# A gate, three edge columns and one step: reordering ScalarE in the opening of a fused forward and backward kernel

## The chip, the cores and the metric

One core of a Trainium2 chip runs the whole kernel. The metric is device time in microseconds, the median of several executions. TensorE (PE in the profile) multiplies matrices and writes to PSUM; ScalarE (ACT) and VectorE (DVE) read PSUM and work elementwise; GpSimd (POOL) and SyncE (SP) mostly issue transfers here. [...]

## The reference

A layer with two branches, mixed by a gate, and its gradients. `x` has 2048 rows of 1024, the inner width `F` is 3584, everything is bfloat16.

```python
g = sigmoid((x * gate_w).sum(-1, keepdims=True))       # one number per row
X = rfft2(x);  a = irfft2(X * (w_r + 1j * w_i))        # spectral branch
h = x @ w1 + b1;  r = relu(h);  b = (r * r) @ w2 + b2  # dense branch
out = g * a + (1 - g) * b
# returned: out and, for a given grad_out, the gradients of
# x, w_r, w_i, w1, b1, w2, b2 and gate_w
```

## The kernel before

The rows are worked on in 16 tiles of 128 rows. In the opening TensorE makes `h` in groups of eight matmuls (`ph`, L747): ScalarE applies Relu (`rT`, L748) and the square (`h2T`, L749). Then it makes the gradient of the square, also in groups of eight (`pd`, L755), which VectorE multiplies with `2 rT` (`dhT`, L759). `ph` and `pd` share two PSUM banks in the opening, so a group of matmuls can start only when the group before the last has been read.

```python
def bank(name):
    drawn[0] += 1
    return banks[drawn[0] // 2 % len(banks)].tile([P, SW], FP32, name=name, tag="ph", bufs=2)

def hidden(fc, ss, w1g, h2T, rT):
    ph = bank("ph")
    for dc in range(DC):                      # eight matmuls
        opened(mm(ph[:], lhsT=w1g[...], rhs=xT[:, dc, ss], ...), fc)
    nc.scalar.activation(rT[:], ph[:], ACT.Relu, bias=b1col[:, fc : fc + 1])
    nc.scalar.activation(h2T, rT[:], ACT.Square)
```

The gate needs one weighted sum for each row. VectorE makes it for each tile as the rows land (`weigh`, L666, into `gsum`). For four tiles at a time ScalarE makes `1 - g` (`omg`) and `g` (`gcol`), and VectorE scales four tiles of the incoming gradient with `omg`, which TensorE then transposes (`turn_grad`, L647) for the gradient products.

```python
def gate(i0):
    c_ = slice(i0, i0 + 4)
    nc.scalar.activation(omg[:, c_], gsum[:, c_], ACT.Sigmoid, scale=-1.0)   # L675
    nc.scalar.activation(gcol[:, c_], gsum[:, c_], ACT.Sigmoid)              # L676
    for i in range(i0, i0 + 4):
        later["scaled"] = nc.vector.tensor_scalar(out=dbn[:, i, :], in0=dbn[:, i, :], scalar1=omg[:, i : i + 1], ...)
        after(later["scaled"], later["copied"], mybir.DependencyClass.NoSync)
```

The spectral branch begins beside all this. Each tile of `x`, loaded once more (`src`), is folded: sums and differences of its halves (`uv`), then of its quarters (`f`). VectorE does the wide parts, ScalarE three narrow copies of edge columns (L263, L265, L269). Then TensorE multiplies along the rows (`pk`, L277) and along the columns (`pu`, L310).

```python
def folds(fb, xt, earlier=None):
    uv = fb.tile([P, 2, H], FDT, name="uv", tag="uv", bufs=2)
    after(V(out=uv[:, 0, :], in0=xt[:, 0:H], in1=xt[:, H:D], op=ALU.add), earlier, mybir.DependencyClass.NoSync)
    after(V(out=uv[:, 1, :], in0=xt[:, 0:H], in1=xt[:, H:D], op=ALU.subtract), earlier, mybir.DependencyClass.NoSync)
    f = fb.tile([P, 6, Q + 2], FDT, name="f", tag="f", bufs=2)
    ...                                                                        # L261, L262: VectorE
    nc.scalar.copy(out=f[:, 3:0:-2, 0], in_=uv[:, 1, 0 : Q + 1 : Q])           # L263
    nc.scalar.copy(out=f[:, 0:3:2, 0 : Q + 1 : Q], in_=uv[:, 0:1, 0 : Q + 1 : Q].to_broadcast([P, 2, 2]))   # L265
    ...                                                                        # L267, L268: VectorE
    nc.scalar.copy(out=f[:, 5, P::-P], in_=f[:, 0:3:2, P])                     # L269
    return f

def first_stage_of_x():
    f, ft = {0: folds(f1, xs[0], later["last"])}, {}
    for i in range(NT + 1):
        ...
        ft[i] = row_stage(f1, f[i], kf[:], later["last"]);  yield              # pk
        ...                                                                    # pu of tile i - 1, folds of i + 1
        yield
```

`after(a, b, NoSync)` tells the scheduler that `a` comes after `b`; no semaphore is added. The scheduler then chooses the order on each engine. The opening is 32 units, four blocks of eight: eight groups `ph` for rows 0 to 1023, eight groups `pd`, and the same for rows 1024 to 2047.

```python
for u in range(32):
    for i in before.get(u, ()): turn_x(i)               # holds the row sums
    for i in grads_before.get(u, ()): turn_grad(i)
    next(units)                                         # one group ph or pd
    if u in (6, 15, 19):
        gate({6: 4, 15: 8, 19: 12}[u])
    if u == 17:
        for n in range(3): xs[n] = source(n, x_perm)
        stage = first_stage_of_x()
    if u > 19 and u % 2:
        next(stage)
...
total = 22 + 2 * (NT + 4) + 14 + 5 + 4 * R1 + 2 + LEAD + 4 * NT    # steps of side work left after the opening
```

In the rest of the kernel the spectral work runs as side work between the large products: its steps are dealt out at a rate that is worked out from `total`.

Of the kernel before, what the change touches and what calls it, by code (L numbers as in the profile page):

```python
# [10 lines left out]
P = 128  # L11
# [4 lines left out]
ACT = mybir.ActivationFunctionType  # L16
# [108 lines left out]
LEAD = 8  # L125
# [15 lines left out]
def kernel(  # L141
# [22 lines left out]
    nc = tc.nc  # L164
# [8 lines left out]
    R1, R2 = g.R1, g.R2  # L173
    NT = S // P
    Q, H, LW, W1 = D // 4, D // 2, g.Df + 1, g.Df
# [18 lines left out]
    def pool(name, side="left", space=SBUF, stack=None, bufs=1):  # L194
        stack = ExitStack() if stack is None else stack
        kw = {} if space == DRAM else dict(side=side, reuse_waits="tile")
        return stack.enter_context(tc.tile_pool(name=name, bufs=bufs, space=space, **kw)), stack
# [10 lines left out]
    gcol, omg, gpg, bGo, dsc = (cols(n, [NT]) for n in ("gcol", "omg", "gpg", "bGo", "dsc"))  # L208
    gsum = cols("gsum", [NT])
# [24 lines left out]
    def after(ins, earlier, wait=mybir.DependencyClass.Sync):  # L234

        if earlier is not None:
            info = mybir.DependencyInfo(wait, mybir.DependencyReason.DATA)
            tc.add_manual_dep(ins.ins, earlier.ins.name, info, reason="paced")
# [12 lines left out]
    tps, tps_s = pool("tps", "right", PSUM)  # L251


    def folds(fb, xt, earlier=None):
        uv = fb.tile([P, 2, H], FDT, name="uv", tag="uv", bufs=2)
        after(V(out=uv[:, 0, :], in0=xt[:, 0:H], in1=xt[:, H:D], op=ALU.add), earlier, mybir.DependencyClass.NoSync)
        after(V(out=uv[:, 1, :], in0=xt[:, 0:H], in1=xt[:, H:D], op=ALU.subtract), earlier, mybir.DependencyClass.NoSync)

        f = fb.tile([P, 6, Q + 2], FDT, name="f", tag="f", bufs=2)
        a0, a1 = uv[:, :, 1:Q], uv[:, :, H - 1 : Q : -1]  # L260
        V(out=f[:, 0:2, 1:Q], in0=a0, in1=a1, op=ALU.add)  # L261
        V(out=f[:, 2:4, 1:Q], in0=a0, in1=a1, op=ALU.subtract)  # L262
        nc.scalar.copy(out=f[:, 3:0:-2, 0], in_=uv[:, 1, 0 : Q + 1 : Q])  # L263

        nc.scalar.copy(out=f[:, 0:3:2, 0 : Q + 1 : Q], in_=uv[:, 0:1, 0 : Q + 1 : Q].to_broadcast([P, 2, 2]))  # L265
        b0, b1 = f[:, 0:3:2, 0:P], f[:, 0:3:2, Q:P:-1]
        V(out=f[:, 4:6, 0:P], in0=b0, in1=b1, op=ALU.add)  # L267
        V(out=f[:, 4:6, P:Q], in0=b0, in1=b1, op=ALU.subtract)  # L268
        nc.scalar.copy(out=f[:, 5, P::-P], in_=f[:, 0:3:2, P])  # L269
        return f  # L270

    def row_stage(fb, f, kmat, earlier=None):
        pk = fps.tile([P, 8, P], FP32, name="pk", tag="ps2", bufs=2)
        even = [(row, slice(o, o + P)) for row, o in ((5, P), (4, 0), (4, P), (5, 0))]
        odd = [(row, slice(o, Q, 2)) for row, o in ((3, 0), (3, 1), (1, 1), (1, 0))]
        for b, (row, o) in enumerate(even + odd):
            first_ = mm(pk[:, b, :], lhsT=f[:, row, o], rhs=kmat[:, b // 6, :], start=True, stop=True)  # L277
            if b == 0:
                after(first_, earlier, mybir.DependencyClass.NoSync)
        ft = fb.tile([P, 8, P], FDT, name="ft", tag="ft", bufs=2)  # L280
        nc.scalar.copy(out=ft[:], in_=pk[:])
        return ft

    def first_columns(fb, cf, T, i, ft, earlier=None):
        pu = fps.tile([P, 2, H], FP32, name="pu", tag="ps2", bufs=2)
        column_stage(pu, ft, cf, earlier)

        u = fb.tile([P, D], FDT, name="u", tag="u", bufs=2)
        w = fb.tile([P, 2, 2, 2, P // 2], FDT, name="w", tag="w", bufs=2)
        nc.scalar.copy(out=w[:].rearrange("p c x g i -> p (c x g i)"), in_=pu[:, 1, :])  # L290
        uv = u[:].rearrange("p (c h g i) -> p c h g i", c=2, h=2, g=4)
        even = pu[:, 0, :].rearrange("p (g c h i) -> p c h g i", g=2, c=2, h=2)
        nc.scalar.copy(out=uv[:, 0, :, 0::2, :], in_=even[:, 0])
        nc.scalar.mul(out=uv[:, 1, :, 0::2, :], in_=even[:, 1], mul=flip[:])  # L294

        X, Y = (w[:, :, x] for x in range(2))
        V(out=uv[:, :, 0, 1::2, :], in0=X, in1=Y, op=ALU.add)
        V(out=uv[:, :, 1, 3::-2, ::-1], in0=X, in1=Y, op=ALU.subtract)
        rows_of(st, z_scr, T, i, u, True)
# [325 lines left out]
    later = {}  # L625
    f1, f1_s = pool("f1", "right")

    cf = f1.tile(list(consts["cf"].shape), FDT, name="cf", tag="cf")
    xs = {}
# [5 lines left out]
    def source(i, view, earlier=None, tag="src"):  # L635
        src = f1.tile([P, D], BF16, name=tag, tag=tag, bufs=8 if tag == "xsrc" else 4)
        loaded = ld(out=src[:], in_=view[i])
        if earlier is None:
            queued(loaded)
        after(loaded, earlier)  # L640
        return src
# [30 lines left out]
    def gate(i0):  # L672

        c_ = slice(i0, i0 + 4)
        nc.scalar.activation(omg[:, c_], gsum[:, c_], ACT.Sigmoid, scale=-1.0)  # L675
        nc.scalar.activation(gcol[:, c_], gsum[:, c_], ACT.Sigmoid)  # L676
        for i in range(i0, i0 + 4):
            later["scaled"] = nc.vector.tensor_scalar(out=dbn[:, i, :], in0=dbn[:, i, :], scalar1=omg[:, i : i + 1], scalar2=None, op0=ALU.mult)
            after(later["scaled"], later["copied"], mybir.DependencyClass.NoSync)

    def first_stage_of_x():
        f, ft = {0: folds(f1, xs[0], later["last"])}, {}
        for i in range(NT + 1):
            if i + 3 < NT:
                xs[i + 3] = source(i + 3, x_perm, later["last"])
            if i < NT:
                ft[i] = row_stage(f1, f[i], kf[:], later["last"])
                yield
            if i > 0:
                first_columns(f1, cf, 0, i - 1, ft[i - 1], later["last"])  # L690
            if i + 1 < NT:
                f[i + 1] = folds(f1, xs[i + 1], later["last"])
            yield
# [23 lines left out]
    def mlp_in():  # L717
# [9 lines left out]
# [3 lines that stand above are left out]
# [9 lines left out]
        def opened(ins, fc):  # L739
            if fc < 4:  # L740
                after(ins, later["turned"], mybir.DependencyClass.NoSync)
                later["product"] = ins

        def hidden(fc, ss, w1g, h2T, rT):
            ph = bank("ph")
            for dc in range(DC):
                opened(mm(ph[:], lhsT=w1g[:, dc, fc % 2 * P : (fc % 2 + 1) * P], rhs=xT[:, dc, ss], start=(dc == 0), stop=(dc == DC - 1)), fc)  # L747
            nc.scalar.activation(rT[:], ph[:], ACT.Relu, bias=b1col[:, fc : fc + 1])  # L748
            nc.scalar.activation(h2T, rT[:], ACT.Square)  # L749

        def grads(fc, sb, ss, rT, dhT):
            w_ = w2T[fc // FGC]
# [936 lines left out]
    def turn_x(i):  # L1689
        if i >= NT // 2:  # L1690
            weigh(i, rows.pop(i), later["copied"])
            return
        turn_tile(xT, i, rows[i], nc.vector.tensor_copy if i in (1, 3) else nc.scalar.copy, later["gate_row"] if i == 2 else later.get("product"))
        if i >= 3:
            for n in range(4 if i == 3 else 1):
                weigh(n if i == 3 else i, rows.pop(n if i == 3 else i), later["copied"] if i == 3 else None)

    def turn_grad(i):
        turn_tile(dbT, i, dbn[:, i, :], nc.vector.tensor_copy, later["product"])
# [27 lines left out]
    for i in range(4):  # L1727
        turn_x(i)
        warm((0, 2, 2, 0)[i])
        if i == 1:  # L1730
            vectors(vrow)
    gate(0)
    next(units)
    rows_of_grad(1)
# [10 lines left out]
    for u in range(32):  # L1745
        for i in before.get(u, ()):
            turn_x(i)
        for i in grads_before.get(u, ()):
            turn_grad(i)
        next(units)  # L1750
        if u in (6, 15, 19):
            gate({6: 4, 15: 8, 19: 12}[u])
        if u == 17:
            for n in range(3):
                xs[n] = source(n, x_perm)
            stage = first_stage_of_x()
        if u > 19 and u % 2:
            next(stage)
    V(out=gpg[:], in0=gcol[:], in1=omg[:], op=ALU.mult)
    later["more_banks"]()  # L1760
# [42 lines left out]
        pass  # L1803
    grads = mlp_grads()
    next(grads), next(grads)
    total = 22 + 2 * (NT + 4) + 14 + 5 + 4 * R1 + 2 + LEAD + 4 * NT
    todo = total - 2 * 12

    def rate():
# [46 lines left out]
```

## Time and profile before

| | |
|---|---|
| median of three | 1207.06 us (1205.73 to 1207.61) |
| profiled execution | 1206.89 us, span of the profile 1205.1 us |
| granted TensorE clock, mean | 0.998 |
| TensorE idle in the span | 22.3 us |
| opening: the 32 units | about 10 to 83 us |

How to read it: an engine's "idle before" is the time in which it had nothing running just before an instruction, and the arrow names what released it. The names left of the arrow in an instruction are what it writes, right of it what it reads. A group with "x8" is eight such instructions, its duration from the start of the first to the end of the last.

### The profile page before, as it was taken

To read this page: it belongs to the slowest core of one execution; us is meant where nothing else is said; L and a number is where in the kernel's file an instruction comes from. 1 tells how busy PE (TensorE), PEld (TensorE's weight loads), DVE (VectorE), ACT (ScalarE), POOL (GpSimd) and SP (SyncE) were. 2 spreads that over 40 slices of the span, in tenths; PEclk is the share of its full clock that TensorE was granted. 3 is DMA by queue.
4 is the path that set the end of the run, shared out by engine and by line. 5 is a ranking of instruction groups with operands and counts; after the bars stand their busy time and mean duration, and the time that the engine had idled before them with its cause. 6 is when DMAs were issued, how large, how long until landed. Compare 5 with 4: busy or idle time off the path is not lost.

```text
span 1205.1 us, 19779 instructions
## 1 busy us (share of the span) xinstructions
PE 1182.8 (98%) x7055; PEld 647.7 (54%) x7149; DVE 845.4 (70%) x1842; ACT 614.4 (51%) x1121; POOL 365.5 (30%) x587
## 2 busy tenths in 40 slices
PE   9899999999999999999999999999999999999998
PEld 5455545544444444444447888888544544444444
DVE  5766546676878887877789846665489866966464
ACT  6257757755777863444444425554455523232322
POOL 1024434413455451433333353545132100000000
PEclk9999999999999999999999999999999999999999
DMA  9957576686757598999999799976976699965551
GB/s 273 288 160 206 137 203 191 165 166 183 208 171 208 180 231 169 188 202 226 226 189 188 179 214 200 209 202 197 283 212 178 195 206 249 246 203 173 158 152 35
DMA packets 341104, 236.53 MB, mean 196 GB/s; under 512 B 206237, under 2 KB 299963, under 8 KB 341004
## 3 DMA queue, kind: packets, MB, share of 16 engines
q1 hardware_dynamic: 309552, 144.08, 54.0%
q0 software_dynamic: 30224, 90.61, 24.8%
q8 instruction: 56, 0.92, 0.3%
q10 hardware_dynamic: 1228, 0.57, 0.2%
q14 instruction: 44, 0.36, 0.1%
HBM read 107.24 MB, written 81.81 MB: 157 GB/s over the span
## 4 chain that ended last, share of the span: by engine, by line
PE 88%; DVE 4%; DMA 4%; ACT 2%; issue 1%; POOL 0%; SPq 0%; ACTq 0%; DVEq 0%
PE pd L755 15%; PE ph L747 15%; PE pX L1378 13%; PE pV L1378 10%; PE pX L947 8%; PE pX L1023 6%; PE pV L947 6%; PE pV L1023 5%; PE acc L1475 2%; PE pu L310 2%; PE pk L277 1%; PE px L416 1%; DMA xsrc<-in_A_x_dram 1%; DMA r<-y_scr 1%; PE pv L447 1%
## 5 line engine op out<-in xcount | busy, mean ns | idle before, releaser
L747 PE MATMUL ph<-xT,w1g 128*128 128x512 bf16 x867 | 216.0, 381 | 7.3 <-ACT rT L748 4.5
L755 PE MATMUL pd<-dbT,w2T 128*128 128x512 bf16 x876 | 209.5, 379 | 0.9
L755 PEld LDWEIGHTS <-w2T 128*128 128x128 bf16 x896 | 87.1, 98 | 102.9
L747 PEld LDWEIGHTS <-w1g 128*128 128x128 bf16 x896 | 85.6, 98 | 99.1 <-issue 6.5
L759 DVE SCALAR_TENSOR_TENSOR dhT<-pd,rT 128x512 bf16<-128x512 f32 x108 | 74.3, 688 | 77.8 <-PE pd L755 62.8
L748 ACT ACTIVATE rT<-ph,b1col 128x512 bf16<-128x512 f32 x108 | 74.5, 690 | 49.1 <-PE ph L747 46.3
L1023 PEld LDWEIGHTS <-res 128*128 128x128 bf16 (+1 forms) x896 | 86.7, 98 | 11.7 <-issue 0.8
L1378 PEld LDWEIGHTS <-dS 128*128 128x128 f16 x588 | 57.2, 98 | 66.0 <-issue 0.7
L226 POOL DMA_DIRECT2D r<-y_scr x96 | 58.4, 613 | 102.7 <-ACT re L553 56.0
L419 ACT CAST x<-px 64x512 f16<-64x512 f32 x128 | 74.2, 580 | 27.1 <-PE px L416 26.0
L226 POOL DMA_DIRECT2D z_scr<-u x96 | 58.6, 617 | 92.0 <-ACT u L294 48.0
L1023 PEld LDWEIGHTS <-X 128*128 128x128 f16 x672 | 64.9, 98 | 7.9
L749 ACT ACTIVATE h2T<-rT 128x512 bf16<-128x512 bf16 x108 | 67.9, 628 | 2.3
L1378 PEld LDWEIGHTS <-odd 128*128 128x128 bf16 (+1 forms) x392 | 38.2, 98 | 45.3
L1378 PEld LDWEIGHTS <-even 128*128 128x128 bf16 (+1 forms) x392 | 38.0, 98 | 44.3
L456 POOL DMA_DIRECT2D y_scr<-pc x64 | 36.1, 565 | 63.1 <-DVE pc L453 60.3
L947 PEld LDWEIGHTS <-S 128*128 128x128 f16 x336 | 32.8, 98 | 39.7 <-DVE S L921 0.3
L394 POOL COPY w<-wn 128x512 bf16<-128x512 bf16 x32 | 24.3, 760 | 90.7 <-DVE tt L427 73.4
L1400 DVE TENSOR_TENSOR cu<-pV,u 128x512 f16<-128x512 f32 x27 | 18.6, 690 | 40.9 <-PE pV L1378 34.8
L1351 POOL DMA_DIRECT2D out_dram<-gxo x14 | 7.6, 540 | 130.8 <-DVE gxo L1350 130.8
L1378 PE MATMUL pX<-wT,dS 128*128 128x512 f16 x196 | 44.6, 379 | 0.0
L810 POOL DMA_DIRECT2D h2T_scr<-h2T x28 | 20.7, 740 | 75.5 <-ACT h2T L749 42.0
(275 smaller groups left out, 2471.4 us busy)
## 6 DMA issues: line engine op xcount, KB each, us to landing
h2T_scr<-h2T POOLq DMA_DIRECT2D x28, 512.0 KB, 4.2
dhT_scr<-dhT POOLq DMA_DIRECT2D x28, 512.0 KB, 5.9
z<-z_scr SPq DMA_DIRECT2D x64, 128.0 KB, 3.2
y_scr<-pc POOLq DMA_DIRECT2D x64, 128.0 KB, 4.0
ax_scr<-yo POOLq DMA_DIRECT2D x32, 256.0 KB, 5.3
out_dram<-whi POOLq DMA_DIRECT2D x28, 256.0 KB, 5.6
out_dram<-wlo POOLq DMA_DIRECT2D x28, 256.0 KB, 5.3
even<-h2T_scr SPq DMA_DIRECT2D x8, 896.0 KB, 6.2
```

The source lines that it names most:

```text
L226: issue(out=a, in_=b) if stored else issue(out=b, in_=a)
L394: G.tensor_copy(out=w[:, 0:2, 0:HW].rearrange("p c (g i) -> p c g i", g=4), in_=wn[:, :, h * HW : (h + 1) * HW].rearrange("p c (i g) -> p ...
L419: nc.scalar.copy(out=x[lanes[n], c, :, 0:HW], in_=px[lanes[c], n])
L456: st(out=y_scr[:][c, :, :, h].rearrange("r x t l -> (r x) t l"), in_=pc[:, n])
L747: opened(mm(ph[:], lhsT=w1g[:, dc, fc % 2 * P : (fc % 2 + 1) * P], rhs=xT[:, dc, ss], start=(dc == 0), stop=(dc == DC - 1)), fc)
L748: nc.scalar.activation(rT[:], ph[:], ACT.Relu, bias=b1col[:, fc : fc + 1])
L749: nc.scalar.activation(h2T, rT[:], ACT.Square)
L755: opened(mm(pd[:], lhsT=w_[:, ec, fc % FGC * P : (fc % FGC + 1) * P], rhs=dbT[:, ec, ss], start=(ec == 0), stop=(ec == DC - 1),), fc)
L759: return STT(out=dhT, in0=pd[:], scalar=2.0, in1=rT[:], op0=ALU.mult, op1=ALU.mult, accum_out=gb1part[:, fc, sb : sb + 1],)
L947: self.mm = mm(acc[:], lhsT=lhs[:, t, c_], rhs=rhs[:, t, :], start=start and t == 0, stop=t == KH - 1, skip_group_check=True,)
L1023: ins = mm(acc[:, j * FH : (j + 1) * FH], lhsT=lhs[:, t, c_], rhs=rhs[:, t, :], start=start and first_ is None, stop=t == KH - 1, skip_gro ...
L1378: pe(mm(acc[:], lhsT=lhs[:, c, :], rhs=rhs[:, c, :], start=start and c == 0, stop=c == KH - 1, skip_group_check=True,))
```

## The change

It rearranges ScalarE's order in the second forward block of the opening, so that small instructions that wait for late data come behind the large ones that free PSUM banks. The gate's first instruction gets an order behind the square made last, and the last gate is asked for two units later. The first fold is ordered behind the latest copy of a turned tile, its two first edge columns behind the latest square. The side stage is stepped from unit 23 on and no longer from 21, and the count of steps that are left is one higher. Nothing is computed differently.

```diff
-    def folds(fb, xt, earlier=None):
+    def folds(fb, xt, earlier=None, copies=None):
@@ in folds
-        nc.scalar.copy(out=f[:, 3:0:-2, 0], in_=uv[:, 1, 0 : Q + 1 : Q])
-
-        nc.scalar.copy(out=f[:, 0:3:2, 0 : Q + 1 : Q], in_=uv[:, 0:1, 0 : Q + 1 : Q].to_broadcast([P, 2, 2]))
+        edge = nc.scalar.copy(out=f[:, 3:0:-2, 0], in_=uv[:, 1, 0 : Q + 1 : Q])
+        after(edge, copies, mybir.DependencyClass.NoSync)
+
+        edge = nc.scalar.copy(out=f[:, 0:3:2, 0 : Q + 1 : Q], in_=uv[:, 0:1, 0 : Q + 1 : Q].to_broadcast([P, 2, 2]))
+        after(edge, copies, mybir.DependencyClass.NoSync)
@@ in gate
-        nc.scalar.activation(omg[:, c_], gsum[:, c_], ACT.Sigmoid, scale=-1.0)
+        first_ = nc.scalar.activation(omg[:, c_], gsum[:, c_], ACT.Sigmoid, scale=-1.0)
+        after(first_, later.get("squared"), mybir.DependencyClass.NoSync)
@@ in first_stage_of_x
-        f, ft = {0: folds(f1, xs[0], later["last"])}, {}
+        f, ft = {0: folds(f1, xs[0], later["copied"], later["squared"])}, {}
@@ in hidden
-            nc.scalar.activation(h2T, rT[:], ACT.Square)
+            later["squared"] = nc.scalar.activation(h2T, rT[:], ACT.Square)
@@ the opening
-        if u in (6, 15, 19):
-            gate({6: 4, 15: 8, 19: 12}[u])
+        if u in (6, 15, 21):
+            gate({6: 4, 15: 8, 21: 12}[u])
...
-        if u > 19 and u % 2:
+        if u > 22 and u % 2:
             next(stage)
...
-    total = 22 + 2 * (NT + 4) + 14 + 5 + 4 * R1 + 2 + LEAD + 4 * NT
+    total = 23 + 2 * (NT + 4) + 14 + 5 + 4 * R1 + 2 + LEAD + 4 * NT
```

## The prediction

> **What bounds the kernel now.** I read the table of busy time first, then the waits of TensorE over the whole span, then the three compute engines as timelines around the one large wait, and last the granted clock microsecond by microsecond.
>
> ```profile
> PE 1182.8 (98%) x7055; PEld 647.7 (54%) x7149; DVE 845.4 (70%) x1842; ACT 614.4 (51%) x1121; POOL 365.5 (30%) x587
> ```
>
> TensorE is busy 98% of a span of 1205.1 us: only 1205.1 - 1182.8 = 22.3 us are idle, and a change that removes no matmul can only win from those, or from matmuls that ran at a low clock. The waits of TensorE by releaser (total, times, longest):
>
> ```profile
> PE ph L747 <- ACT rT L748: 4.5, 1, 4.5
> PE pki L566 <- DVE rf L558: 1.9, 4, 0.7
> ```
>
> The first row is one wait, the largest of the run, and the change is aimed at it. TensorE around it (start, duration, instruction, count, idle before):
>
> ```profile
> 50.45 1.89 PE L747 MATMUL ph<-xT,w1g 128*128 128x512 bf16 x7
> 52.17 0.61 PE L647 MATMUL pt<-identb,dbn 128*128 128x128 bf16 x8
> 57.33 3.57 PE L747 MATMUL ph<-xT,w1g 128*128 128x512 bf16 x8 [4.55 <-ACT rT L748]
> 60.70 0.65 PE L277 MATMUL pk<-kf,f 128*128 128x128 f16 x8
> ```
>
> The group at 57.33 is the sixth product of the second forward pass. It takes the bank of the fourth (two banks alternate), which had been finished at about 50.1 and waited for its Relu. Why the Relu was late stands in ScalarE's timeline:
>
> ```profile
> 48.47 0.69 ACT L748 ACTIVATE rT<-ph,b1col 128x512 bf16<-128x512 f32 x1 [0.38 <-PE ph L747]
> 53.55 0.21 ACT L675 ACTIVATE omg<-gsum 128x4 f32<-128x4 f32 x1 [4.39 <-DVE gsum L666]
> 53.66 0.19 ACT L676 ACTIVATE gcol<-gsum 128x4 f32<-128x4 f32 x1
> 53.76 0.61 ACT L749 ACTIVATE h2T<-rT 128x512 bf16<-128x512 bf16 x1
> 56.50 0.20 ACT L263 COPY f<-uv 128x2 f16<-128x2 f16 x1 [2.13 <-DVE uv L257]
> 56.60 0.68 ACT L748 ACTIVATE rT<-ph,b1col 128x512 bf16<-128x512 f32 x1
> ```
>
> So two small instructions stand in the queue ahead of the fourth Relu: the last gate, held until the last row sum (4.39 us), and the first edge column of the fold, held until the fold (2.13 us). VectorE shows that both waits are in the end transfers:
>
> ```profile
> 48.85 1.23 DVE L666 CUSTOM_DVE_ANT_0 uv<-xsrc,gwb 128x1024 f16<-128x1024 bf16 x1 [3.83 <-DMA xsrc<-in_A_x_dram]
> ...
> 53.44 0.08 DVE L666 DVE_READ_ACCUMULATOR2_ANT gsum<- 128x1 f32 x1
> 55.70 0.42 DVE L256 TENSOR_TENSOR uv<-src 128x512 f16<-128x512 bf16 x1 [2.19 <-DMA src<-in_A_x_dram]
> ```
>
> The last row sum is ready at 53.52 whatever TensorE does: four sums of about 1.15 us one after another, from a landing at 48.8. The clock (window, its length, the busy time of the five engines, granted clock, DMA share, GB/s):
>
> ```profile
> 56.00:57.00 1.00, 0.00 (x0) 0.00 (x0) 1.00 (x4) 0.50 (x2) 0.00 (x0) 1.00 0.56 101
> ...
> 58.00:59.00 1.00, 1.00 (x4) 0.31 (x3) 1.00 (x4) 0.00 (x0) 0.00 (x0) 0.50 0.84 159
> 59.00:60.00 1.00, 1.00 (x4) 0.45 (x3) 1.00 (x4) 0.65 (x2) 0.00 (x0) 0.50 1.17 249
> ...
> 61.00:62.00 1.00, 1.00 (x17) 0.82 (x15) 0.81 (x5) 0.27 (x2) 0.00 (x0) 1.00 0.57 198
> ```
>
> After the gap the matmuls run at half clock until about 60.7. The eight of this group took from 57.33 to 60.70, 3.37 us, against 1.73 for such a group on the chain elsewhere: 1.64 us lost beside the 4.55.
>
> [...] the gap of 4.55 us was followed by 3.4 us at 0.50, the gap of 1.02 us near 9 us by none. [...] here the small ones start 0.10 apart though each lasts 0.2. So the small instructions themselves cost about 0.1 us each, and only their waits matter.
>
> **The change part by part.** No instruction is added or removed, only order, so I compared the order of the two built programs on each engine.
>
> (1) *The edge columns of the first fold.* They stood before the fourth, fifth and sixth Relu; now all three come behind the eighth square. The Relus no longer wait for the fold: the hold from 53.76 to 56.60 goes.
>
> (2) *The last gate.* Only its first half, `omg`, gets the new dependency. In the new order the second half, `gcol`, has not followed it: it stands alone behind the third Relu and ahead of the third square, where the whole gate was, and it needs the same row sum. So the hold until 53.5 stays. Then: `gcol` at 53.55, third square 0.10 later at 53.65, fourth Relu 0.53 after that (the distance from a square to the next instruction at 17.64 and 18.17) at 54.18, done at 54.86, and TensorE goes on 0.05 later (57.33 against 56.60 + 0.68) at 54.91. Saved: 57.33 - 54.91 = 2.42 us; a gap of about 2.1 us is left.
>
> (3) *The clock.* [...] I expect no drop: 1.64 us saved.
>
> (4) *The first fold comes later.* From the end of the eighth product TensorE has one tile of transposes (0.45 to the next start) and one gradient product (1.73) and then stands at the first `pk`, 2.18 us later. What `pk` needs is a chain over two engines: Relu 0.72 up to the square, square 0.53, two edges 0.10 and 0.21, two VectorE additions 0.21 and 0.30, the last edge column 0.20, and five handovers of about 0.05 to 0.10: about 2.6 to 2.7. New wait: about 0.5 us.
>
> (5) *The second gate.* The dependency is in the shared helper, so `omg` of tiles 4 to 7 moves as well, from 20.35 to behind the seventh square, about 26.8. The scaling of tile 4 then ends at about 27.5, where its weight load started at 27.28 before: up to 0.2 us. But TensorE runs from there into the gap, whose end is set by a transfer, so the gap swallows it: 0.
>
> (6) *The side work is dealt one step later* (five steps in the opening and not six; the total of the rate goes from 22 to 23). In the row stage the pattern with seven gradient matmuls, `pk`, and the eighth takes 4.73 us a turn (`pk` at 112.46 and 117.19), the other 4.42 (86.73 and 91.15). The order has six of the first kind after, five before: +0.3. In the gradient's row stage the slow kind (4.62, `pk` at 175.15 and 179.77) goes from eight to six, at 0.2 each: -0.4. Together about 0. Later stages hold idle time of their own (1.5 us between 880 and 900, 0.7 to 0.8 near 750, 810 and 910), and their pieces are shuffled too; I can't read a sign, and allow 1.5 us either way.
>
> Sum: -2.42 - 1.64 + 0.5 + 0 + 0 = -3.56 us, and 1207.06 - 3.56 = 1203.5.
>
> **The rivals.** *The whole wait goes.* If the fourth Relu ran at 50.15 there would be no gap: -4.55 - 1.64 + 0.5 = -5.7, or 1201.4. The words of the change ("last gate behind the sixth square") speak for it; against it is the place of `gcol` in the order, which the program shows plainly. *The clock still drops.* [...] then -2.42 + 0.5 = -1.9, or 1205.1. The gap of 1.02 us, with transposes ahead of it and no drop, speaks against it, but it is shorter. *The gain is given back.* A new stall at `pk` longer than I think, or late stages that meet their `pki` waits (1.9 us over four in the row above) more often: with +1.5 on top, 1205, and in the worst case no difference. For it speaks that nearly every engine's order differs from here to the end; against it, that the work is the same and TensorE takes what is ready with 98% busy.
>
> **Range and chances.** The middle is 1203.5. The low end is the whole wait gone with nothing lost later, 1201.0 with the scatter of the runs; the high end is the dropped clock with 1.5 us lost later, 1206.6. The runs before spread from 1205.73 to 1207.61, which is inside what I allow. Two per cent is 24 us, more than all of TensorE's idle time (22.3), so faster by that much is out of reach short of an error: 0.01. Slower by 24 us would need a new serial wait in every stage: 0.01. Within: 0.98.
>
> **What would show it right or wrong.** Step 2: in the changed profile ScalarE idles some 4.4 us ahead of one `gcol` near 53.5, the fourth Relu starts near 54.2, and TensorE's wait for L748 is about 2.1 and not 4.5. Step 3: the windows from 55 to 62 show clock 1.00 throughout. Step 4: a wait of about 0.5 us of TensorE for L269 ahead of the first `pk`, near 63. Step 5: the second `omg` near 26.8 and no lasting shift. Step 6: idle time outside 50 to 64 stays within 1.5 us of what it was. The prediction is wrong if there is no gap at all there (then `gcol` did not hold the queue), if the clock dips in spite of the short gap, or if the opening gains its 3.5 us and the end of the span doesn't move.

## The result, and the profile after

The changed kernel takes **1213.18 us** (median of four, 1211.62 to 1215.86) against 1207.05 us for the kernel before, measured beside it: a ratio of 1.0055, with a 95% interval of 1.0035 to 1.0075. It is slower by about 6 us. The prediction was 1203.5 us, in a range that ended at 1206.6, so it had the wrong sign. Lines of the changed file stand two or three further down than before: `ph` L750, `rT` L751, `h2T` L752, `gcol` L679, `dhT` L762.

The table of busy time, for a span of 1211.9 us:

```profile
PE 1183.3 (98%) x7054; PEld 647.5 (53%) x7149; DVE 846.3 (70%) x1842; ACT 615.7 (51%) x1121; POOL 360.6 (30%) x587
```

TensorE's work is the same within 0.5 us (1182.8 before), but it is idle 1211.9 - 1183.3 = 28.6 us, and was idle 22.3. The waits of TensorE by releaser (total, times, longest) name them:

```profile
PE ph L750 <- ACT rT L751: 2.5, 1, 2.5
PE px L418 <- DMA ab<-c_ab: 1.9, 1, 1.9
...
PE pX L950 <- DVE S L924: 1.4, 1, 1.4
PE pd L758 <- DVE dhT L762: 1.3, 4, 0.5
PE pV L950 <- DVE even L924: 1.2, 1, 1.2
...
PE pki L568 <- DVE rf L560: 1.2, 3, 0.7
...
PE pV L1026 <- DVE wlo L961: 0.8, 1, 0.8
```

The first row is the wait at which the change aims; it fell from 4.5 to 2.5. The rows for `px`, `S`, `dhT`, `even` and `wlo` are **new**: 1.9 + 1.4 + 1.3 + 1.2 + 0.8 = 6.6 us, none of them in the opening.

In the opening itself the order on ScalarE came out as worked out beforehand (start, duration, instruction, idle before):

```profile
48.88 0.69 ACT L751 ACTIVATE rT<-ph,b1col 128x512 bf16<-128x512 f32 x1 [0.38 <-PE ph L750]
54.37 0.20 ACT L679 ACTIVATE gcol<-gsum 128x4 f32<-128x4 f32 x1 [4.81 <-DVE gsum L668]
54.48 0.61 ACT L752 ACTIVATE h2T<-rT 128x512 bf16<-128x512 bf16 x1
55.00 0.67 ACT L751 ACTIVATE rT<-ph,b1col 128x512 bf16<-128x512 f32 x1
```

`gcol` alone holds the queue until the last row sum; nothing of the fold stands behind it any more. On TensorE:

```profile
55.72 3.54 PE L750 MATMUL ph<-xT,w1g 128*128 128x512 bf16 x8 [2.54 <-ACT rT L751]
59.08 0.62 PE L649 MATMUL pt<-identb,dbn 128*128 128x128 bf16 x8
```

The group after the gap took 59.08 - 55.72 = 3.36 us where 1.73 is normal. The clock (last but two of the columns) did fall:

```profile
55.00:56.00 1.00, 0.28 (x1) 0.10 (x1) 0.54 (x1) 0.97 (x3) 0.00 (x0) 0.84 1.19 365
56.00:57.00 1.00, 1.00 (x4) 0.35 (x3) 0.00 (x0) 0.97 (x3) 0.00 (x0) 0.50 1.23 151
...
59.00:60.00 1.00, 1.00 (x12) 0.68 (x11) 0.26 (x1) 0.69 (x1) 0.00 (x0) 0.95 0.36 26
```

To place the rest I compared the start of the same square (`h2T`) in two traces, at 461 us the last `dhT` of the hidden-layer part, and after it the same copies of the products; "end" is the last of them. The numbers are us against the trace of the kernel before; a column is named by the time in the kernel before. "Start" is the first square: a lag there is a later start of the run's data and no effect of the order.

| trace | start 13 | 103 | 256 | 280 | 440 | 461 | 478 | end |
|---|---|---|---|---|---|---|---|---|
| the change | +0.40 | -0.57 | -1.19 | +0.11 | -0.37 | +2.33 | +5.37 | +6.69 |

The opening's gain is used up by 280 us, and then the run loses twice: between 440 and 461, and between 461 and 478. This led to the theory for the experiments.

**Theory S (step).** The loss comes from the part that I had put at "about 0": the side work is dealt one step later for the rest of the kernel. **Rival O (order).** The new ScalarE order itself costs later, for instance through a fold that comes late or gates that let transfers collide.

### The profile page after: what moved, and what is told of

It is laid out like the page before. It is cut to its first block, busy times and chain, and to the rows that moved or that the text cites. A ratio compares the mean times of both kernels' runs of the same rounds, so it can differ in the third digit from the quotient of the medians.

```text
span 1211.9 us, 19773 instructions
## 1 busy us (share of the span) xinstructions
PE 1183.3 (98%) x7054; PEld 647.5 (53%) x7149; DVE 846.3 (70%) x1842; ACT 615.7 (51%) x1121; POOL 360.6 (30%) x587
## 4 chain that ended last, share of the span: by engine, by line
PE 83%; DVE 8%; ACT 3%; issue 3%; DMA 3%; ACTq 0%; POOL 0%; DVEq 0%; SPq 0%; POOLq 0%
PE pd L758 13%; PE pX L1381 13%; PE ph L750 13%; PE pV L1381 9%; PE pX L950 7%; PE pX L1026 7%; PE pV L1026 5%; PE pV L950 5%; PE acc L1478 2%; PE pu L312 1%; PE pk L279 1%; PE pki L568 1%; PE pv L449 1%; PE pui L312 1%; PE px L418 1%
## 5 line engine op out<-in xcount | busy, mean ns | idle before, releaser
L750 PE MATMUL ph<-xT,w1g 128*128 128x512 bf16 x867 | 215.8, 381 | 5.7 <-ACT rT L751 2.5
L750 PEld LDWEIGHTS <-w1g 128*128 128x128 bf16 x896 | 85.7, 98 | 97.7 <-issue 4.5
L762 DVE SCALAR_TENSOR_TENSOR dhT<-pd,rT 128x512 bf16<-128x512 f32 x108 | 74.2, 688 | 74.5 <-PE pd L758 64.6
L751 ACT ACTIVATE rT<-ph,b1col 128x512 bf16<-128x512 f32 x108 | 74.6, 691 | 59.3 <-PE ph L750 56.3
L752 ACT ACTIVATE h2T<-rT 128x512 bf16<-128x512 bf16 x108 | 67.9, 629 | 2.3
L428 DVE TENSOR_TENSOR tt<-x,w 128x1028 f16<-128x1028 f16 (+1 forms) x32 | 22.2, 695 | 36.2 <-issue 14.3
```

The lines of the kernel that those rows point to most:

```text
L752: later["squared"] = nc.scalar.activation(h2T, rT[:], ACT.Square)
L762: return STT(out=dhT, in0=pd[:], scalar=2.0, in1=rT[:], op0=ALU.mult, op1=ALU.mult, accum_out=gb1part[:, fc, sb : sb + 1],)
```

## The experiments

Four kernels were run together. In them the two parts of the change are separated.

**step_only**: the kernel before with the later step alone.

```diff
-        if u > 19 and u % 2:
+        if u > 22 and u % 2:
-    total = 22 + ...
+    total = 23 + ...
```

> The kernel before with only the two numbers of the side work changed: first step at unit 23 and not 21, total 23 and not 22; gate and folds as before. Theory S (the loss is the side work that lies one step behind from the opening on: its pieces then fall on other products in every later stage): the opening keeps its 4.5 us wait and its dip of the clock, and the later stages lose what they lost in the changed kernel, about 7 to 8 us (the changed kernel lay 1.6 us ahead at 256 us, its slower start left out, and 6.7 behind at the end): 1214 to 1215 us. Rival O (the new order of ScalarE in the opening is what costs later): 1207.

Measured: 1213.47 us, against 1207.62 for the kernel before in the same set; ratio 1.0052 (1.0033 to 1.0070). The step alone brings the whole loss.

**no_step**: the changed kernel with those two lines as they were; the new ScalarE order alone.

> The changed kernel with the two numbers put back: first step at unit 21, total 22; the gate's and folds' new order stays. From the end of the opening on every engine's order is that of the kernel before. Theory S: the opening's gain stays (wait 2.5 and not 4.5, clock still dips) and nothing is lost later: about 1205.4. Rival O: still about 1213.

Measured: 1203.81 us, ratio 0.9966 (0.9952 to 0.9980). The order alone wins 3.8 us. Rival O falls. That this is close to the 3.56 predicted for the whole is partly luck. I expected the gap of 2.5 us and the drop of the clock to stay (1205.4); in this trace the last row sum ended at 51.9 and not at 53.5, since its rows had landed earlier, the gap was 0.4 us and the clock stayed. The opening won 5.2 us, and 3.8 of them went again between 750 and 815 us, in waits of `pki` for `rt` (2.1) and `rf` (1.4) and of `pX` for `G` (1.0) that `rejoin`, with the same late order, doesn't have. Why they appear isn't known.

**rejoin**: the changed kernel, with the missing step made up in the first unit after the opening, so that all later orders are those of the kernel before.

```diff
-    for _ in spread(units, spec, first_rate):
+    for _ in spread(units, spec, first_rate, 1.0):
```

> The changed kernel, with one step of side work more at the start of the later units, so that the missing step of the opening is made up at once and all later steps fall on the units on which they fell before. Opening as in the changed kernel. Theory S: about 1205.4, and the waits near 260 to 284, 443 and 473 to 477 us gone. Rival O: about 1213.

Measured: 1203.36 us, ratio 0.9968 (0.9956 to 0.9979). Its trace has none of the five new waits. So it isn't the later step in the opening that costs, but staying one step behind afterwards. It is 2 us faster than expected; in its trace the gap was 1.72 us and the clock stayed.

**both_rejoin**: `rejoin`, and the second half of the gate follows the square too.

```diff
-        nc.scalar.activation(gcol[:, c_], gsum[:, c_], ACT.Sigmoid)
+        second_ = nc.scalar.activation(gcol[:, c_], gsum[:, c_], ACT.Sigmoid)
+        after(second_, later.get("squared"), mybir.DependencyClass.NoSync)
```

> As the run with the step made up, and the gate's second half (gcol) ordered behind the square as well as its first. If gcol alone holds ScalarE's queue and so TensorE: the fourth Relu runs near 50.2 us, TensorE's wait for it and the dip of the clock vanish, 4.5 + 1.6 us less than before, with 0.3 for the first pk: about 1201.2. If something else (transfers of the gradient rows, the last row sums) holds the opening anyway: a new wait of 2 us or more near 55 to 60 and about 1204 to 1205.

Measured: 1202.80 us, ratio 0.9958 (0.9944 to 0.9972). The gap in the opening is gone, as ScalarE shows: the fourth Relu runs at 50.38, and the gate's two halves wait for nothing.

```profile
50.38 0.69 ACT L752 ACTIVATE rT<-ph,b1col 128x512 bf16<-128x512 f32 x1 [0.38 <-PE ph L751]
...
55.98 0.19 ACT L677 ACTIVATE omg<-gsum 128x4 f32<-128x4 f32 x1
56.08 0.19 ACT L679 ACTIVATE gcol<-gsum 128x4 f32<-128x4 f32 x1
```

It is the fastest median of this study, though its interval overlaps that of `rejoin`, and it is 1.6 us above the 1201.2 that I expected. The table below shows why the two end alike in their traces: `both_rejoin` leads by 1.6 us up to 478 and gives it back in the last part, where the `pki` wait for `rf` grew from 2.0 to 3.4 us.

The second set asks where staying behind costs, and whether it is the direction that counts.

**rejoin_late**: the changed kernel, with the step made up at the end of the hidden-layer part, just before the weight-gradient products.

```diff
     for _ in spread(units, spec, first_rate):
         pass
+    next(spec, None)
```

> The changed kernel, with the missing step of side work made up only at the end of the hidden-layer part (near 460 us), just before the weight-gradient products begin; from there on every engine has the order of the kernel before. Theory 'two places': the loss has one part before it (near 256 to 284 us, where TensorE waits for dhT, about 1.5 us) and one after it (the change of stage near 461 to 478 and the stretch to 700, together about 4 us). Then the run lies near 1208.5 us (1207 to 1210): TensorE still waits for dhT four times near 260 to 283, but the waits of pV and pX for even and S near 472 to 481 are gone. Theory 'late only': everything is lost after 460, and the run is as fast as the one with the step made up early, 1203 to 1204.5. Theory 'early only': the order in the hidden-layer part does it all, and the run stays at 1212 to 1214.

Measured: 1212.28 us (1208.68 to 1219.32), ratio 1.0044 (1.0027 to 1.0061). 'Two places' is missed, and by its number 'early only' is met. But the trace shows that my kernel didn't separate what it should: it keeps the waits near 472 that I had expected to vanish, and only what comes after 478 us is as before (+4.53 at 478, +4.40 at the end).

```profile
PE pd L758 <- DVE dhT L762: 1.6, 4, 0.9
...
PE pX L950 <- DVE S L924: 1.4, 1, 1.4
```

A step made up at the change of stage puts its pieces there as well. That made the point for `rejoin_pause`.

**both_halves**: the changed kernel with the second half of the gate tied, and the step still missing.

> The changed kernel with the second half of the gate (gcol) ordered behind the square as well; the side work stays one step late. Theory: the opening then wins all of its gap (about 4.5 us instead of 2.0) and keeps the clock (1.6 us more), as it did in the run that also makes the step up, but the later loss of about 9 us stays. From 1202.8 with the step made up: 1202.8 + 9.5 to 10 = 1212 if the late loss is independent of the opening, and no better than 1209 in any case. Rival (the late loss is a matter of how early the transfers and VectorE stand against TensorE, so of the opening itself): the run goes to 1203 to 1206.

Measured: 1213.53 us, ratio 1.0042 (1.0027 to 1.0058). The opening wins all of its gap, and nothing is left of it at the end: the late loss is larger than in `step_only`. One wait took the gain back:

```profile
441.64 1.03 PE L418 MATMUL px<-pm,ab 128*128 128x512 f16 x2 [2.86 <-DMA ab<-c_ab]
442.47 3.00 PE L751 MATMUL ph<-xT,w1g 128*128 128x512 bf16 x8
```

TensorE waits 2.86 us for the load of `ab`, and then both groups run slow (1.03 and 3.00 us; 0.59 and 1.89 are usual). In `step_only`, where TensorE comes later, the same `px` starts at 442.52 without a wait.

**ahead**: the kernel before with the side work one step earlier (the edit of `rejoin` in the kernel before).

> The kernel before with the side work dealt one step EARLIER from the first unit after the opening; the opening itself is the old one. Theory 'a tuned deal': the interleaving was tuned step by step, and a shift either way meets new waits: 1209 to 1214. Theory 'late is bad': only being behind costs, because sums and edge pieces then stand ahead of the work of the next stage; a step ahead gives 1205 to 1208, the old time or a little better.

Measured: 1207.17 us, ratio 1.0012 (0.9992 to 1.0031): no difference that the interval can tell from none, though it leaves room for 3.7 us, and four of the 14 executions took 1213.0 to 1219.6, where the kernel before, in 24, took 1211.3 at most. One step behind costs 5.9 us; for one step ahead no cost is shown.

**behind2**: the kernel before with two steps less in the opening.

```diff
-        if u > 19 and u % 2:
+        if u > 24 and u % 2:
-    total = 22 + ...
+    total = 24 + ...
```

> The kernel before with the side work TWO steps later (stepped from unit 25 on, total 24), gates and edges untouched. One step later alone gave 1213.5 against 1207.6. Theory 'each step behind moves the loss further': 1216 to 1222. Theory 'a phase': the loss comes from which pieces happen to meet at the change of stage, so two steps give another number that needn't be larger, anywhere from 1206 to 1214.

Measured: 1218.68 us, ratio 1.0101 (1.0064 to 1.0138): +10.9 us for two steps after +5.9 for one. The six executions lie in two groups, though, 1214.2 to 1215.6 and 1221.8 to 1228.1, and the median falls between them: two steps seem to cost more than one (the intervals just overlap), but that each costs about as much isn't shown. In the trace, of 1221.76 us, the wait for `even` is 3.2 us and the one for `wlo` 2.3, for 1.2 and 1.0 in `step_only`.

The last two take the loss apart at the pause: the last five units of the hidden-layer part deal no side work.

**rejoin_pause**: the changed kernel, with the missing step made up in the last unit before the pause.

```diff
-        return 0.0 if left_[0] < 6 else 1.6 if "mid" in later else 1.75
+        return 0.0 if left_[0] < 6 else 2.6 if left_[0] == 6 else 1.6 if "mid" in later else 1.75
```

> The changed kernel, with the missing step made up in the last unit that deals side work in the hidden-layer part, ahead of the pause of five units before the weight-gradient products (near 445 us). Made up behind the pause it left 1212.3 us, and TensorE still waited for S and even near 472 and 476. Theory 'the piece behind the pause': that loss of about 3 us comes from side pieces that stand in VectorE's queue ahead of the first sums, so ahead of the pause the step costs nothing: the two waits are gone, and the run lies 3 us under the one before, at 1208 to 1210 (the early part, 1.5 to 2 us at dhT, stays). Rival (the change of stage is late because TensorE and VectorE arrive in another phase, wherever the step is made up): the waits stay and the run is again near 1212.

Measured: 1207.28 us (1207.13 without the execution of 1223.87), against 1206.85 for the kernel before; ratio 1.0004 (0.9991 to 1.0018). A little faster than expected, perhaps because the opening kept its clock in its trace (gap 1.49 us). The waits for `S` and `even` are gone and those for `dhT` stay, as the theory has it.

**drop_pause**: the opposite. `rejoin`, with one step less in the last unit before the pause (0.6 in place of 2.6 in that line).

> The opposite: the version with the step made up at once (1203.4 us), but with one step less in the last unit that deals before the pause, so that everything up to there is in the old order and everything behind it in the order of the changed kernel. Theory 'the parts add up': it loses what the changed kernel loses from 461 us on, 3 us at the change of stage and 1 to 1.5 in the weight-gradient part, and nothing at dhT near 260 to 283: 1207 to 1208.5. Theory 'the part before the pause does it': 1203 to 1204.5.

Measured: 1207.65 us, ratio 0.9999 (0.9983 to 1.0015), as expected. Its waits of TensorE contain nothing for `dhT`, but again:

```profile
PE pX L950 <- DVE S L924: 1.4, 1, 1.4
PE pV L950 <- DVE even L924: 1.2, 1, 1.2
```

Against the kernel before in their own sets, `rejoin` gains 4.26 us; with the early part behind (`rejoin_pause`) it is +0.28, with the late part behind (`drop_pause`) +0.80. The early part thus costs 4.5 and the late part 5.1 us, 9.6 together; from `rejoin` (-4.26) to the change (+6.13) are 10.4. By the ratios, which are of means, the parts are 4.3 and 3.7, 8.1 of 10.5, and each ratio is known to 1.4 to 2.4 us. So both parts cost, and add up to most of the loss. The one trace of `rejoin_pause` shows only 1.8 us for the early part; its executions of 1209.4 to 1213.2 us have a lower granted clock (0.996 to 0.998) than those up to 1207.2 (0.999 to 1.000), and where they lose it isn't recorded. All traces in one table, as above:

| trace | start 13 | 103 | 256 | 280 | 440 | 461 | 478 | end |
|---|---|---|---|---|---|---|---|---|
| step_only | +0.32 | +0.80 | +0.16 | +1.55 | +1.30 | +1.96 | +4.99 | +6.55 |
| both_halves | +2.55 | -2.71 | -3.21 | -1.89 | -2.60 | +2.58 | +5.61 | +7.33 |
| ahead | +0.52 | +0.75 | -0.86 | -0.45 | +1.58 | +0.24 | +0.24 | -1.11 |
| behind2 | +2.25 | +0.81 | +2.03 | +3.75 | +4.56 | +3.33 | +8.54 | +14.88 |
| rejoin_late | +0.70 | +0.36 | -0.27 | +1.55 | +0.84 | +1.49 | +4.53 | +4.40 |
| drop_pause | +0.50 | -2.81 | -2.81 | -2.81 | -2.81 | -3.25 | -0.23 | +0.68 |
| rejoin_pause | +0.82 | -2.81 | -3.45 | -1.36 | -2.07 | -0.97 | -0.97 | -1.03 |
| rejoin | +0.06 | -3.21 | -3.21 | -3.20 | -3.21 | -3.21 | -3.21 | -3.57 |
| both_rejoin | +0.12 | -5.02 | -5.02 | -5.02 | -4.77 | -4.77 | -4.77 | -3.56 |
| no_step | +0.18 | -5.03 | -5.04 | -5.03 | -4.86 | -4.86 | -4.86 | -1.09 |

## Why the prediction was wrong

**Step 6 failed**, the side work dealt one step later: "Together about 0 ... I can't read a sign, and allow 1.5 us either way." I counted two patterns in the row stages and stopped there. The runs put +5.9 us on that step alone with the old order and about +9.9 with the new one (from -3.8 for `no_step` to +6.1 for the change, each against the kernel before of its own set). Being behind matters where VectorE is full (busy for 22.7 of the 23 us from 260 to 283 in the changed trace), or where one stage hands over to the next.

*Near 260 to 283 us* VectorE adds up the rows of the gradient (L1770) between the `dhT` that TensorE waits for. VectorE in the changed kernel:

```profile
278.66 1.22 DVE L1770 TENSOR_TENSOR even<-even,dbn 128x1024 f32<-128x1024 f32 x1
279.91 1.25 DVE L1773 STREAM_TRANSPOSE even<-even 128x1024 f32<-128x1024 f32 x1
281.19 1.22 DVE L1775 TENSOR_REDUCE even<-even 128x32 f32<-128x1024 f32 x1
282.32 0.68 DVE L762 SCALAR_TENSOR_TENSOR dhT<-pd,rT 128x512 bf16<-128x512 f32 x1
...
283.54 0.17 DVE L354 COPY ed<-ed 64x64 f16<-64x64 f16 x1
```

and TensorE waiting for it:

```profile
283.07 1.67 PE L758 MATMUL pd<-dbT,w2T 128*128 128x512 bf16 x7 [0.46 <-DVE dhT L762]
```

An add, the transpose and the reduction stand in one block of 3.7 us ahead of a `dhT`. In `rejoin` a `dhT` stands between the transpose and the reduction, and TensorE waits for no `dhT`:

```profile
273.63 1.25 DVE L1773 STREAM_TRANSPOSE even<-even 128x1024 f32<-128x1024 f32 x1
274.80 0.65 DVE L762 SCALAR_TENSOR_TENSOR dhT<-pd,rT 128x512 bf16<-128x512 f32 x1
275.38 0.08 DVE L762 DVE_READ_ACCUMULATOR dhT<-pd,rT 128x1 f32 x1
275.38 1.22 DVE L1775 TENSOR_REDUCE even<-even 128x32 f32<-128x1024 f32 x1
```

There are four such waits, 1.3 us together (1.6 in `step_only`).

*Near 441 us* the load of `ab` is issued in another place. SyncE's queue in the kernel before, and then in the changed one:

```profile
426.99 0.53 SPq L378 DMA_DIRECT2D ab<-c_ab  x1
427.57 7.73 SPq L181 DMA_TRANSPOSE even<-h2T_scr  x2
```

```profile
432.05 4.98 SPq L181 DMA_TRANSPOSE even<-h2T_scr  x1
437.13 1.15 SPq L380 DMA_DIRECT2D ab<-c_ab  x1
```

Behind the transposing transfers it leaves at 437.13 and lands 5.7 us later (the longest; the median of the `ab` loads is 2.6), while `px` could have run at 441.02. A late landing alone doesn't cost: in the kernel before the same load took 7.0 us, but it had left 10.1 us earlier, and its `px` came at 436.68 without a wait. `px` waited 1.9 us here and 2.9 in `both_halves`, and not at all in `step_only` and `rejoin_late`, whose TensorE comes at 442.1 to 442.5. So the more the opening wins, the more is lost here. From 440 to 461 us the change loses 2.7 us and `both_halves` 5.2, for 0.7 in `step_only`: in these traces the place is worth 2.0 and 4.5 us. That it makes up the whole difference between the medians, +5.9 and +9.9, is not shown; no run took it out by itself.

*Near 461 to 478 us* the weight-gradient products begin, and VectorE must make their sums (`T`, `S`, `even`). In the changed kernel:

```profile
464.94 0.08 DVE L762 DVE_READ_ACCUMULATOR dhT<-pd,rT 128x1 f32 x1
465.05 0.42 DVE L441 TENSOR_TENSOR y<-tt 64x512 f16<-64x512 f16 x1
...
467.56 0.42 DVE L442 TENSOR_TENSOR y<-tt 64x512 f16<-64x512 f16 x1
468.01 2.29 DVE L898 TENSOR_TENSOR T<-dbn 128x4096 f16<-128x4096 bf16 x1
```

Six side pieces stand between the last `dhT` and the first sum, 468.01 - 464.94 = 3.07 us. TensorE has work for a part of this and then stands twice:

```profile
473.23 1.90 PE L950 MATMUL pV<-T,even 128*128 128x512 f16 x8 [1.25 <-DVE even L924]
476.57 1.90 PE L950 MATMUL pX<-T,S 128*128 128x512 f16 x8 [1.44 <-DVE S L924]
```

together 2.69 us, and the table's step from 461 to 478 is 3.04. In `rejoin_pause` the pieces have gone ahead of the pause and the sum follows the last `dhT` at once:

```profile
461.02 0.69 DVE L762 SCALAR_TENSOR_TENSOR dhT<-pd,rT 128x512 bf16<-128x512 f32 x1 [2.75 <-PE pd L758]
461.63 0.08 DVE L762 DVE_READ_ACCUMULATOR dhT<-pd,rT 128x1 f32 x1
461.63 2.29 DVE L898 TENSOR_TENSOR T<-dbn 128x4096 f16<-128x4096 bf16 x1
```

The first line shows that VectorE idled 2.75 us shortly before: there was room for the pieces, but not where they stood in the queue. *After 478 us* another 1.3 us go (waits for `wlo`, 0.8, and others), which `rejoin_late`, back in the old order there, doesn't have. Which piece does it isn't settled.

**Step 1** was right: no Relu waits for the fold.

**Step 2** was right in its mechanism: `gcol` at 54.37, for 53.55 worked out, since the last row sum came later in this run (read out at 54.26, after VectorE had waited 0.69 us for `xsrc` between two sums); the wait fell by 2.0 us, for 2.42. That sum isn't fixed, as I had taken it to be: it ended at 51.9 in `no_step` and at 55.2 in `step_only`, with the landing of its rows. `both_rejoin` shows the other side of it: with `gcol` tied as well there is no gap.

**Step 3** failed in the measured trace. I took a gap of about 2.1 us for too short to drop the clock. That was an assumption of mine: the trace before shows a drop after its gap of 4.55 us, none after those of 1.02 to 1.18, and no gap of a length between. A gap of 2.54 us dropped it, and 1.63 of the 1.64 us stayed lost (other gaps in the last section). The rival "The clock still drops" was the truth here, and the middle of my range should not have counted this gain in full: the gap ends with a landing that varies from trace to trace, and `rejoin`, with the same order, had 1.72 us and no drop (its group took the usual 1.89 us):

```profile
54.61 1.89 PE L750 MATMUL ph<-xT,w1g 128*128 128x512 bf16 x8 [1.72 <-ACT rT L751]
```

**Step 4**: the first `pk` waited 0.25 us, for about 0.5. **Step 5** was right: the second `omg` moved to 27.12, and no lasting shift follows.

The sum for the changed trace: -2.0 (gap) + 0 (clock) + 0.25 (`pk`) = -1.8 in place of -3.56. To come to +6.1 the side work must have cost 6.1 + 1.8 = 7.9 us, and its new waits listed above are 6.6. (The table has 0.97 won by 103 us and 7.3 lost after it, the later start taken off.) "The gain is given back" was the right rival, but with the "+1.5 on top" I gave it a fifth of its size.

## What to carry to other kernels

A change that is local on one engine can shift a dealt schedule for the rest of the kernel; take the shift out first (`rejoin` is one argument) and judge the local part by itself. Side work that fell behind cost here at the hand-over between stages, where six of its pieces stood in VectorE's queue for 3.07 us ahead of the first sum of the next stage, and time saved upstream went into the wait for a load that was issued late (1.9 us in the change, 2.9 in `both_halves`); a step ahead cost nothing that could be measured here (ratio 1.0012, 0.9992 to 1.0031). When reading an order for such a change, don't count patterns in the steady stages: look at what stands ahead of the first instruction of each new stage, on each engine.

## What the runs showed of the hardware

The clock fell after a shorter gap than I had expected. Seven gaps of TensorE were each followed by a clock of 0.50: 2.54 us (the change), 2.86 (`both_halves`), 3.12 (`rejoin_late`), 3.23 and 3.42 (`behind2`), 3.39 (`ahead`) and 4.55 (the kernel before). Where the windows cover the whole drop, after 4.55, 2.54, 2.86 and 3.23 us, it lasted 3.4 us. After shorter gaps the clock stayed at 1.00: 1.02 us (the kernel before, near 9 us), 1.45 (`rejoin_late`, near 10), 1.49 (`rejoin_pause`), 1.54 and 1.66 (`drop_pause`, near 10 and 55) and 1.70 (the change, near 10). Between them it went both ways: 1.82 us (`both_halves`, near 10 us) and 2.06 us (`behind2`, near 11 us) dropped it, 1.82 us (`no_step`), 1.87 us (the change, near 442 us) and 2.11 us (`no_step`, near 756 us) did not. So between 1.8 and 2.1 us the length of the gap alone didn't decide here; what else did isn't shown.

In `behind2` the clock falls three times, after 2.06, 3.42 and 3.23 us:

```profile
11.00:12.00 1.00, 1.00 (x5) 0.43 (x4) 1.00 (x3) 0.00 (x0) 0.00 (x0) 0.86 1.06 387
...
59.00:60.00 1.00, 1.00 (x5) 0.42 (x4) 1.00 (x4) 1.00 (x2) 0.00 (x0) 0.75 1.30 187
...
475.00:476.00 1.00, 0.00 (x0) 0.00 (x0) 1.00 (x2) 0.00 (x0) 1.00 (x1) 0.96 1.04 319
```

Transposes stand ahead of the gaps of 2.54 and 4.55 us in the opening. The gap of 2.86 us in `both_halves` comes straight behind a group of eight large matmuls (436.89, 1.89 us), and the clock fell too:

```profile
440.00:441.00 1.00, 0.00 (x0) 0.00 (x0) 0.87 (x4) 0.00 (x0) 0.00 (x0) 1.00 1.05 352
441.00:442.00 1.00, 0.36 (x1) 0.13 (x2) 0.00 (x0) 0.00 (x0) 0.00 (x0) 0.64 0.87 285
442.00:443.00 1.00, 1.00 (x4) 0.41 (x3) 0.29 (x1) 0.29 (x1) 0.00 (x0) 0.50 0.49 155
```

Where the cost of a drop was worked out, it was some 1.6 us beside the gap (1.63 in the change, 1.5 in `both_halves`).
